# Attention output token-major with a ones column, and one common pool of PSUM banks, in a fused linear-attention and gated-MLP kernel

## The chip, the cores and the metric

The kernel runs on one core of a Trainium2 chip. The metric is the device time of one execution in microseconds (us). The kernel before took 319.83 us (median of three runs, 319.49 to 319.84) when the prediction was made.

The engines go by the names of the profile: PE is TensorE, which multiplies matrices (PEld is its loading of weights), DVE is VectorE, ACT is ScalarE, POOL is GpSimd. Of the two operands of a matmul, the one that is loaded as weights is called stationary here, the other moving. PSUM (PS in the profiles) is the memory that the matmuls of this kernel write to; the kernel uses it as eight banks.

## The reference, cut to what matters

```python
xn = layernorm(x)                                  # x: 2048 tokens x 640
q, k, v = split(xn @ wqkv)                         # 32 heads of 20
pq, pk = q @ w_phi, k @ w_phi                      # per head, 20 x 20
phi_q = concat(softmax(pq), softmax(-pq))          # same for phi_k with pk
kv = phi_k^T @ v ;  z = sum over tokens of phi_k   # per head
o = (phi_q @ kv) / (phi_q @ z + 1e-6)
out = x + o @ wo + (silu(xn @ w1) * (xn @ w3)) @ w2    # hidden width 1536
```

There are two halves that share the normalised tokens: a linear attention, and a gated MLP that is by far the larger part of the matmul work.

## The kernel before

The program is written as *streams* of steps: norms, attention, k normalisations, MLP, output tiles. When it is built, a small recorder looks at the head of every stream, estimates with its own costs when each could start, and commits the one that could start first; ties go to the earlier stream. The result is a fixed order of instructions on each engine, with semaphore waits.

The step that normalises k is a DVE reduction and reciprocal, and two POOL multiplications. The kv sums need all of them:

```python
def k_norm(t):                                         # (cut: the names of views)
    P.op("DVE", "tensor_reduce", [s], [e], ...)        # sums of exp over each head
    P.op("DVE", "reciprocal", [r], [s], ...)
    for sg in range(2):                                # sg: exp(pk), exp(-pk)
        tt("POOL", ev, ev, r[...].to_broadcast(...), ALU.mult)

def kv_sum(sg, fc, k):                                 # (cut: h0, h1, nh, the heads of this chunk)
    for t in range(T):
        mm(bank(k, 21 * nh), ekt[:, t, sg, fc * 128:(fc + 1) * 128],
           v2[:, t, 21 * h0:21 * (h1 + 1)], t == 0, t == T - 1)
    # ... masked copies of the result into KVc (kv) and ZG (z)
```

The attention output works on 512 tokens with channels on the partitions. The softmax sums and the denominators are found token-major, turned around, spread over the channels by a matmul with a 0/1 matrix (GT2), and multiplied onto exp(pq) before the product with kv:

```python
def q_sums(b, k):
    for j in range(4):
        for sg in range(2):
            for fc in range(DC):
                mm(bank(k, 64, 128 * j + 64 * sg), EqT[...][:, sg, fc, 128 * j:128 * j + 128],
                   ZG[:, sg, fc, :], fc == 0, fc == DC - 1)
    # ... DVE: products, sum, reciprocal, g_s
def q_scale_t(b, k):                       # four transposes of g_s, ACT copy to gT
def q_scale(b, fc, k):
    for r, sg in ((0, 1), (1, 0)):
        mm(bank(k + r), GT2[32 * r:32 * r + 32, ...], gT[32 * r:32 * r + 32, b % 2, :], True, True)
    for r, sg in ((0, 1), (1, 0)):
        tt("DVE", e, e, bank(k + r), ALU.mult)          # 128 x 512
def q_out(b, dc, k):                       # 26 matmuls of 512 columns for a block
    for n, (sg, fc) in enumerate(plan):
        mm(bank(k), KVc[:, sg, fc, dc * 128:(dc + 1) * 128], EqT[b % 2][:, sg, fc, :], ...)
```

The eight PSUM banks are two rings of four, A for the attention and M for the MLP and the output tiles:

```python
def banks(stream, n):
    base, size = {"A": (0, 4), "M": (4, 4)}[stream]
    # ... next n banks of that ring
```

An MLP chunk is ten matmuls of 512 columns, a tanh on ACT and two operations on DVE. There are 48 chunks; block 2 may be computed before the kv sums, block 3 only after them (its output lies over data that the kv sums read):

```python
while done["t"] < 4 * b + 4 or b == 2 and done["t"] < T or b == 3 and not done["kv"]:
    yield None
yield lambda b=b, fc=fc: mlp(b, fc, banks("M", 2))
```

The softmax here doesn't subtract the row's maximum and nothing guards it: scores larger than these inputs give would overflow.

## Time and profile before

| engine | busy, us of 316.6 | share |
|---|---|---|
| PE (matmuls) | 300.7 | 95% |
| DVE | 177.6 | 56% |
| ACT | 118.5 | 37% |
| POOL | 67.2 | 21% |

First, the page of the kernel before: the span, the busy time of each engine, and the chain of work that ended last, by engine and line with shares of the span.

```profile
span 316.6 us, 4949 instructions
...
PE 300.7 (95%) x2088; PEld 178.8 (56%) x2114; DVE 177.6 (56%) x292; ACT 118.5 (37%) x195; POOL 67.2 (21%) x89
...
PE 94%; DMA 2%; ACT 1%; DVE 1%; issue 1%; SPq 0%
```

The chain is TensorE from end to end. Whether its engine is really never idle is read in the table of waits of PE: who it waited for, in total, how many times, and the longest.

```profile
PE PS L101 <- DVE x_tok L101: 8.3, 2, 5.9
PE PS L101 <- ACT v_84 L101: 1.5, 3, 0.5
PE PS L101 <- ACT ekt L101: 1.1, 1, 1.1
...
PE PS L101 <- DVE ZG L101: 0.2, 1, 0.2
```

Apart from the load of the first tokens there are about 3 us of waits. So the time is the sum of the matmuls, and the sizes that count are distances from start to start. They are read in the timeline (start, length, what, how many; PS is PSUM, w_s the MLP weights, xnT the normalised tokens turned around, Wqp and Wkp the weights of the q and k projections), because the length of a row includes the tail of its last matmul. For that reason the busy time of PE is not a measure of closeness to a limit either; the Trainium skill, "Trainium Kernel Development and Optimization", "Performance Expectations", says so ("a bad metric"), and this trace agrees: one 512-column matmul is listed with 379 ns, while ten of them take 2.16 us.

```profile
144.06 10.83 PE L101 MATMUL PS<-v_84,ekt 128*128 128x147 bf16 x160
154.72 0.43 PE L101 MATMUL PS<-ZG,EqT_74 128*128 128x64 bf16 x9
...
182.39 1.33 PE L101 MATMUL PS<-ZG,EqT_80 128*128 128x64 bf16 x40
183.77 5.34 PE L101 MATMUL PS<-xnT,Wqp 128*128 128x512 bf16 x24
...
191.65 0.60 PE L101 MATMUL PS<-gT,GT_51 32*128 32x512 bf16 x4
192.19 4.49 PE L101 MATMUL PS<-xnT,w_s 128*128 128x512 bf16 x19
...
257.11 5.56 PE L101 MATMUL PS<-EqT_80,KVc 128*128 128x512 bf16 x25 [0.16 <-issue]
262.51 1.52 PE L101 MATMUL PS<-wo_s,oT 128*128 128x320 bf16 x10
```

The reader sees 10.66 us for the 160 kv sums (66.6 ns each), 1.38 us for the forty z matmuls of a block, 0.54 us for four scale matmuls, and 5.40 us for the 26 output matmuls of a block (one record is missing in that row).

### The profile page before, as it was taken

How to read it: one execution, taken by the hardware profiler on the slowest of the kernel's cores; microseconds unless marked ns; L12 is line 12 of the kernel's file. 1: busy time of each engine (PE TensorE's matmuls, PEld its weight loads, DVE VectorE, ACT ScalarE, POOL GpSimd, SP SyncE). 2: the span in 40 equal slices, each digit the busy share in tenths (PEclk: the TensorE clock that was granted, in tenths of full speed). 3: DMA queues.
4: the chain of work that ended last, by engine and by line, in shares of the span. 5: the costliest groups of instructions: out<-in, count | busy, mean ns of one | idle time of the engine just before them, and what ended most of it. 6: DMA issues, size and time to landing. Idle time of an engine off the chain costs nothing.

```text
span 316.6 us, 4949 instructions
## 1 busy us (share of the span) xinstructions
PE 300.7 (95%) x2088; PEld 178.8 (56%) x2114; DVE 177.6 (56%) x292; ACT 118.5 (37%) x195; POOL 67.2 (21%) x89
## 2 busy tenths in 40 slices
PE   0799999999999799999999999999999999999996
PEld 0465655555555456448844453454557656777774
DVE  3866476789877877774339538753743651112212
ACT  2476675757444555540172373346030010000000
POOL 4621032447533375990000000000000000000000
PEclk9999999999999999999999999999999999999999
DMA  7996000000000300000360000000011120222211
GB/s 245 339 356 204 2 1 1 3 0 2 0 0 2 97 9 0 1 2 0 93 222 0 0 2 0 0 3 0 3 41 43 49 76 5 80 85 63 63 62 41
DMA packets 15542, 17.38 MB, mean 55 GB/s; under 512 B 1440, under 2 KB 15520, under 8 KB 15520
## 3 DMA queue, kind: packets, MB, share of 16 engines
q1 hardware_dynamic: 15520, 17.07, 17.0%
q8 instruction: 16, 0.26, 0.3%
q14 instruction: 6, 0.05, 0.0%
HBM read 14.44 MB, written 2.62 MB: 54 GB/s over the span
## 4 chain that ended last, share of the span: by engine, by line
PE 94%; DMA 2%; ACT 1%; DVE 1%; issue 1%; SPq 0%
PE PS L101 94%; DMA x_tok<-in_A_x_dram 2%; ACT v_84 L101 1%; ACT ekt L101 0%; SPq L113 0%; DVE bst L101 0%; DVE xres L101 0%; DVE x_tok L101 0%; DVE KVc L101 0%; DVE mv L101 0%; DVE ZG L101 0%
## 5 line engine op out<-in xcount | busy, mean ns | idle before, releaser
L101 PE MATMUL PS<-xnT,w_s 128*128 128x512 bf16 x460 | 106.5, 379 | 1.1
L101 PEld LDWEIGHTS PS<-xnT,w_s 128*128 128x128 bf16 x480 | 45.3, 98 | 51.0 <-issue 1.3
L101 DVE SCALAR_TENSOR_TENSOR t_66<-th,PS 128x512 bf16<-128x512 f32 x48 | 32.8, 683 | 46.6 <-ACT th L101 46.6
L101 POOL TENSOR_TENSOR ekt<-ekt,rS_60 128x640 bf16<-128x640 bf16 x32 | 39.8, 1269 | 50.2 <-DVE rS_60 L101 50.2
L101 DVE TENSOR_TENSOR xres<-PS,xres 128x640 bf16<-128x640 f32 x16 | 13.2, 824 | 53.8 <-PE PS L101 53.8
L101 ACT ACTIVATE th<-PS 128x512 f32<-128x512 f32 x48 | 28.8, 600 | 32.3 <-PE PS L101 31.8
L101 ACT ACTIVATE ekt<-PS 128x640 bf16<-128x640 f32 x32 | 20.8, 701 | 23.5 <-PE PS L101 23.5
L101 PE MATMUL PS<-wv,xnT 128*128 128x320 bf16 x160 | 25.3, 308 | 2.2 <-ACT ekt L101 1.1
L101 PE MATMUL PS<-Wkp,xnT 128*128 128x320 bf16 x160 | 24.2, 299 | 0.5 <-ACT v_84 L101 0.5
L101 PE MATMUL PS<-wo_s,oT 128*128 128x320 bf16 x160 | 24.4, 299 | 0.0
L101 DVE TENSOR_REDUCE S_59<-ekt 128x64 f32<-128x1280 bf16 x16 | 23.4, 1465 | 0.0
L101 ACT ACTIVATE oT<-PS 128x512 bf16<-128x512 f32 x14 | 8.4, 597 | 40.0 <-PE PS L101 40.0
L101 PEld LDWEIGHTS PS<-wv,xnT 128*128 128x128 bf16 x160 | 15.9, 101 | 10.5 <-ACT v_84 L101 1.4
L101 PE MATMUL PS<-xnT,Wqp 128*128 128x512 bf16 x96 | 21.4, 379 | 0.2
L101 PEld LDWEIGHTS PS<-Wkp,xnT 128*128 128x128 bf16 x160 | 15.5, 98 | 8.7 <-ACT v_84 L101 0.7
L101 PEld LDWEIGHTS PS<-wo_s,oT 128*128 128x128 bf16 x160 | 15.3, 98 | 7.2 <-issue 0.8
L101 DVE BATCH_NORM_STATS2 bst<-x_tok 128x6 f32<-128x320 bf16 x32 | 15.3, 479 | 4.5 <-DMA x_tok<-in_A_x_dram 3.9
L101 ACT ACTIVATE v_84<-PS 128x640 bf16<-128x640 f32 x16 | 11.3, 707 | 15.5 <-PE PS L101 15.4
L101 PEld LDWEIGHTS PS<-xnT,Wqp 128*128 128x128 bf16 x100 | 9.5, 98 | 11.1
L101 PE MATMUL PS<-ident,x_tok 128*128 128x128 bf16 x80 | 7.6, 230 | 8.3 <-DVE x_tok L101 8.3
L101 PE MATMUL PS<-w_s,hT_75 128*128 128x320 bf16 x96 | 13.7, 299 | 0.0
L101 PE MATMUL PS<-w_s,hT_76 128*128 128x320 bf16 x96 | 13.7, 299 | 0.0
(75 smaller groups left out, 342.7 us busy)
## 6 DMA issues: line engine op xcount, KB each, us to landing
w_s<-in_B_w_dram SPq DMA_DIRECT2D x6, 640.0 KB, 10.2
xres<-in_A_x_dram SPq DMA_DIRECT2D x16, 160.0 KB, 2.4
out_dram<-xres SPq DMA_DIRECT2D x16, 160.0 KB, 1.8
x_tok<-in_A_x_dram SPq DMA_DIRECT2D x3, 640.0 KB, 8.8
w_s<-in_B_w_dram SPq DMA_DIRECT2D x1, 1920.0 KB, 7.9
wqk_s<-in_A_wqkv_dram SPq DMA_DIRECT2D x2, 800.0 KB, 8.7
wv<-in_A_wqkv_dram SPq DMA_DIRECT2D x1, 800.0 KB, 4.8
wo_s<-in_A_wo_dram SPq DMA_DIRECT2D x1, 800.0 KB, 4.6
```

The lines of the kernel that those rows point to most:

```text
L101: o = _Op(eng, lambda: m(*args, **kw), r, w, cost)
```

## The change

Its intent is to make the attention output token-major. exp(pq) becomes the stationary operand and kv the moving one, with z and a ones column beside each head, so that numerators, denominators and softmax sums come out of the same matmuls. DVE divides, the two signs are added, and o is turned by five PE transposes. Each output product of 128 tokens needs four PSUM banks at once, so the two rings of banks become one common pool, in which each step takes the group that is estimated to be free first.

```diff
-    def q_sums / q_scale_t / q_scale / q_out      (cut: removed whole)
+    def q_tok(t, k):
+        for sg in range(2):
+            for fc in range(DC):
+                for q in range(2):                       # two halves of the heads, one bank each
+                    ...
+                        mm(bank(k + 2 * sg + q, 22 * (hi - lo), 22 * (lo - 16 * q)),
+                           EqT[b % 2][:, sg, fc, 128 * j:128 * j + 128],
+                           KVc[:, sg, fc, 22 * (lo - h0):22 * (hi - h0)], ...)
+        ...                                              # ACT: two copies of sums and denominators
+        tt("DVE", pr, e[:, 0:2, :], e[:, 2:4, :], ALU.mult)
+        tt("DVE", den, pr[:, 0, :], pr[:, 1, :], ALU.add)
+        P.op("DVE", "reciprocal", [den], [den], (den, den), cost=0.42)
+        tt("DVE", g, e[:, 2:4, :], den..., ALU.mult)
+        tt("DVE", p2..., ps[:, :, :, 0:DH], g..., ALU.mult)            # 1280 elements from PSUM
+        tt("DVE", o_tok[:, t % 3, :], p2[:, 0, :], p2[:, 1, :], ALU.add, 2)
+    def o_transpose(t, k):                               # five transposes, one copy to oT
-    def banks(stream, n):                                # two rings of four
+    def banks(n):
+        def free_at(k): ...                              # estimated end of the last use
+        return min(range(0, 8, n), key=free_at)
-    kv_init, GT2, ZG                                     (cut: zero fills and the 0/1 matrix go)
+    streams = [norms(), attention(), k_norms(), o_transposes(), mlps(), outs()]
```

More of the change, by code (lines that the diff above doesn't have):

```diff
@@ L274, in bass_parallel_sum__linear_kernel_hedgehog__glu_gated_swiglu__prompt_kernel @@
     GM = new("GM", [128, DC, H], bf)
-    GT2 = new("GT2", [64, D], bf)
     phi_s = new("phi_s", [128, DC, DH], bf)
@@ L282, in bass_parallel_sum__linear_kernel_hedgehog__glu_gated_swiglu__prompt_kernel @@
     warm = new("warm", [128, 8], f32)
+    pr_s = new("pr_s", [128, 2, 2, H], f32)
+    den_s = new("den_s", [128, 2, H], f32)
+    g_s = new("g_s", [128, 2, 2, H], f32)
     S64 = new("S64", [128, 3, 64], f32)
@@ L296, in bass_parallel_sum__linear_kernel_hedgehog__glu_gated_swiglu__prompt_kernel @@
     wo_s = new("wo_s", [128, DC, D], bf, RX + 12288)
-    ZG = new("ZG", [128, 2, DC, 64], bf, RX + 18688)
     RKV = region(12800)
@@ L312, in bass_parallel_sum__linear_kernel_hedgehog__glu_gated_swiglu__prompt_kernel @@
     EqT1 = new("EqT1", [128, 2, DC, 512], bf, RE + 27648)
-    E_s = new("E_s", [128, 4, 128], f32, RE + 37888)
-    den_s = new("den_s", [128, 4, 32], f32, RE + 39936)
     wqk_s = new("wqk_s", [128, DC, 2 * D], bf, RE + 40960 - 12800)
@@ L320, in bass_parallel_sum__linear_kernel_hedgehog__glu_gated_swiglu__prompt_kernel @@
     oT = new("oT", [128, DC, S], bf, RV)
+    e_s = new("e_s", [128, 2, 4, H], f32, RV + 20480)
     RW = region(12800)
     wqkT = new("wqkT", [128, 2 * DC, D], bf, RW)
-    KVc = new("KVc", [128, 2, DC, D], bf, RW)
+    KVc = new("KVc", [128, 2, DC, 8 * 22], bf, RW)
+    prod = new("prod", [128, 2, 2, D], bf, RW + 3520)
+    o_tok = new("o_tok", [128, 3, D], bf, RW + 8640)
     EqT = [EqT0, EqT1]
-    gT = new("gT", [64, 2, 512], bf, RKV + 10240)
-    g_s = new("g_s", [128, 4, 64], bf, RKV + 12288)
-    pr_s = new("pr_s", [128, 4, 64], f32, RV + 20480)
     PS = nc.alloc_psum_tensor("PS", [128, 8 * 512], f32)
@@ L431, in consts_late @@
         memset("POOL", v2[:].rearrange("p t (h c) -> p t h c", c=21)[:, :, :, DH], 1.0)
-        memset("POOL", GT2[:], 1.0)
-        for r in (0, 32):
-            select(GT2[r:r + 32, :], 0, [[1, D]], -DH, ALU.is_ge, 0.0)
-            select(GT2[r:r + 32, :], DH, [[-1, D]], DH, ALU.is_gt, 0.0)
     def ln_stats(t0, n):
@@ L535, in kv_sum @@
         g = GM[:, fc, h0:h1 + 1]
-        tt("DVE", KVc[:, sg, fc, DH * h0:DH * (h1 + 1)].rearrange("p (h k) -> p h k", k=DH),
-           pv[:, :, 0:DH], g.unsqueeze(2).to_broadcast([128, nh, DH]), ALU.mult)
-        stt(ZG[:, sg, fc, 32 * sg + h0:32 * sg + h1 + 1], pv[:, :, DH],
-            DEN_EPS if sg == 0 else 0.0, g, ALU.add, ALU.mult)
-    def kv_init():
-        memset("POOL", KVc[:], 0.0)
-        memset("POOL", ZG[:], 0.0)
-        copy("POOL", ZG[:, 0, :, 32:64], GM[:])
-        copy("POOL", ZG[:, 1, :, 0:32], GM[:])
+        kv = KVc[:, sg, fc, 0:22 * nh].rearrange("p (h c) -> p h c", c=22)
+        tt("DVE", kv[:, :, 0:DH], pv[:, :, 0:DH], g.unsqueeze(2).to_broadcast([128, nh, DH]), ALU.mult)
+        stt(kv[:, :, DH], pv[:, :, DH], DEN_EPS if sg == 0 else 0.0, g, ALU.add, ALU.mult)
+        copy("POOL", kv[:, :, DH + 1], g)
     def q_proj(b, fc, k):
@@ L553, in q_proj @@
         act(EqT[b % 2][:, 1, fc, :], bank(k), ACT.Exp, -1.0)
-    def q_sums(b, k):
-        for j in range(4):
-            for sg in range(2):
-                for fc in range(DC):
-                    mm(bank(k, 64, 128 * j + 64 * sg), EqT[b % 2][:, sg, fc, 128 * j:128 * j + 128],
-                       ZG[:, sg, fc, :], fc == 0, fc == DC - 1)
-        copy("ACT", E_s[:], bank(k).rearrange("p (j c) -> p j c", c=128))
-        tt("DVE", pr_s[:], E_s[:, :, 0:64], E_s[:, :, 64:128], ALU.mult)
-        tt("DVE", den_s[:], pr_s[:, :, 0:32], pr_s[:, :, 32:64], ALU.add)
-        P.op("DVE", "reciprocal", [den_s[:]], [den_s[:]], (den_s[:], den_s[:]), cost=1.2)
-        tt("DVE", g_s[:].rearrange("p j (s h) -> p j s h", h=32),
-           E_s[:, :, 32:96].rearrange("p j (s h) -> p j s h", h=32),
-           den_s[:].unsqueeze(2).to_broadcast([128, 4, 2, 32]), ALU.mult)
@@ L570, in q_scale_t @@
-    def q_scale_t(b, k):
-        for j in range(4):
-            tr(PSb[0:64, k * 1024 + 128 * j:k * 1024 + 128 * j + 128], g_s[:, j, :])
-        copy("ACT", gT[:, b % 2, :], PSb[0:64, k * 1024:k * 1024 + 512])
-    def q_scale(b, fc, k):
-        for r, sg in ((0, 1), (1, 0)):
-            mm(bank(k + r), GT2[32 * r:32 * r + 32, fc * 128:(fc + 1) * 128],
-               gT[32 * r:32 * r + 32, b % 2, :], True, True)
-        for r, sg in ((0, 1), (1, 0)):
-            e = EqT[b % 2][:, sg, fc, :]
-            tt("DVE", e, e, bank(k + r), ALU.mult)
@@ L584, in q_out @@
-    def q_out(b, dc, k):
-        plan = []
-        for fc in range(DC):
-            h0, h1 = heads_of_chunk(fc)
-            if max(128 * dc, DH * h0) < min(128 * dc + 128, DH * h1 + DH):
-                plan += [(0, fc), (1, fc)]
-        for n, (sg, fc) in enumerate(plan):
-            mm(bank(k), KVc[:, sg, fc, dc * 128:(dc + 1) * 128], EqT[b % 2][:, sg, fc, :],
-               n == 0, n == len(plan) - 1)
-        evac(oT[:, dc, b * 512:(b + 1) * 512], bank(k))
+    def q_tok(t, k):
+        b, j = divmod(t, 4)
+        for sg in range(2):
+            first = [True, True]
+            for fc in range(DC):
+                h0, h1 = heads_of_chunk(fc)
+                for q in range(2):
+                    lo, hi = max(h0, 16 * q), min(h1 + 1, 16 * q + 16)
+                    if lo < hi:
+                        mm(bank(k + 2 * sg + q, 22 * (hi - lo), 22 * (lo - 16 * q)),
+                           EqT[b % 2][:, sg, fc, 128 * j:128 * j + 128],
+                           KVc[:, sg, fc, 22 * (lo - h0):22 * (hi - h0)],
+                           first[q], fc == DC - 1 or (q == 0 and fc == 2), True)
+                        first[q] = False
+        ps = PS[:, k * 512:(k + 4) * 512].rearrange("p (n c) -> p n c", c=512)[:, :, 0:352]
+        ps = ps.rearrange("p n (h c) -> p n h c", c=22)
+        e = e_s[:, t % 2, :, :]
+        for sg in range(2):
+            act(e[:, sg:4 - sg:3 - 2 * sg, :].rearrange("p c (q h) -> p q h c", h=16),
+                ps[:, 2 * sg:2 * sg + 2, :, 20:22], ACT.Copy)
+        pr, den, g = pr_s[:, t % 2, :, :], den_s[:, t % 2, :], g_s[:, t % 2, :, :]
+        tt("DVE", pr, e[:, 0:2, :], e[:, 2:4, :], ALU.mult)
+        tt("DVE", den, pr[:, 0, :], pr[:, 1, :], ALU.add)
+        P.op("DVE", "reciprocal", [den], [den], (den, den), cost=0.42)
+        tt("DVE", g, e[:, 2:4, :], den.unsqueeze(1).to_broadcast([128, 2, 32]), ALU.mult)
+        g = g.rearrange("p s (q h) -> p (s q) h", h=16)
+        p2 = prod[:, t % 2, :, :]
+        tt("DVE", p2.rearrange("p s (q h c) -> p (s q) h c", q=2, c=DH), ps[:, :, :, 0:DH],
+           g.unsqueeze(3).to_broadcast([128, 4, 16, DH]), ALU.mult)
+        tt("DVE", o_tok[:, t % 3, :], p2[:, 0, :], p2[:, 1, :], ALU.add, 2)
@@ L596, in bass_parallel_sum__linear_kernel_hedgehog__glu_gated_swiglu__prompt_kernel @@
+    def o_transpose(t, k):
+        for dc in range(DC):
+            tr(PSb[:, k * 1024 + 128 * dc:k * 1024 + 128 * dc + 128],
+               o_tok[:, t % 3, 128 * dc:128 * dc + 128])
+        src = PSb[:, k * 1024:k * 1024 + D].rearrange("p (c n) -> p c n", n=128)
+        evac(oT[:, :, t * 128:(t + 1) * 128], src)
     nmlp = [0]
@@ L625, in out_tile, with free_at @@
         finish.append(P.dma("SP", out_t[:, t, :], xres[:, t % 4, :]))
-    turn = {"A": 0, "M": 0}
-    def banks(stream, n):
-        base, size = {"A": (0, 4), "M": (4, 4)}[stream]
-        p = turn[stream]
-        if n > 1 and p % n:
-            p += n - p % n
-        turn[stream] = p + n
-        return base + p % size
-    done = dict.fromkeys(("ln", "t", "k", "n", "kv", "o", "h"), 0)
+    def banks(n):
+        def free_at(k):
+            return max([o.end for i in range(k, k + n) for o in P.bank.get(("P", i), {}).values()],
+                       default=0.0)
+        return min(range(0, 8, n), key=free_at)
+    done = dict.fromkeys(("ln", "t", "k", "n", "kv", "q", "o", "h"), 0)
     def norms():
@@ L672, in transposed @@
             yield None
-        yield lambda: xn_transpose(t, banks("A", 1))
+        yield lambda: xn_transpose(t, banks(1))
         done["t"] = t + 1
@@ L680, in attention @@
                 yield from transposed(t + 1)
-            yield lambda t=t: v_tile(t, banks("A", 2))
+            yield lambda t=t: v_tile(t, banks(2))
         for e in range(DC):
-            yield lambda e=e: fold_t(1, e, banks("A", 1))
+            yield lambda e=e: fold_t(1, e, banks(1))
         for dc in range(DC):
-            yield lambda dc=dc: fold_mm(1, dc, banks("A", 2))
+            yield lambda dc=dc: fold_mm(1, dc, banks(2))
         for t in range(T):
-            yield lambda t=t: k_tile(t, banks("A", 2))
+            yield lambda t=t: k_tile(t, banks(2))
             done["k"] = t + 1
@@ L691, in attention @@
             if t >= 4:
-                yield lambda t=t: v_tile(t, banks("A", 2))
+                yield lambda t=t: v_tile(t, banks(2))
             if 4 <= t < 9:
-                yield lambda e=t - 4: fold_t(0, e, banks("A", 1))
+                yield lambda e=t - 4: fold_t(0, e, banks(1))
             if 9 <= t < 14:
-                yield lambda dc=t - 9: fold_mm(0, dc, banks("A", 2))
-        yield kv_init
+                yield lambda dc=t - 9: fold_mm(0, dc, banks(2))
         yield lambda: P.dma("SP", wo_s[:], A_wo.rearrange("(c p) d -> p c d", p=128))
         for fc in range(DC):
-            yield lambda fc=fc: q_proj(0, fc, banks("A", 1))
+            yield lambda fc=fc: q_proj(0, fc, banks(1))
         while done["n"] < T:
@@ L704, in attention @@
             for sg in range(2):
-                yield lambda fc=fc, sg=sg: kv_sum(sg, fc, banks("A", 1))
+                yield lambda fc=fc, sg=sg: kv_sum(sg, fc, banks(1))
         done["kv"] = 1
@@ L709, in attention, with o_transposes @@
         for b in range(NB):
-            yield lambda b=b: q_sums(b, banks("A", 1))
-            if b + 1 < NB:
-                for fc in range(DC):
-                    yield lambda b=b, fc=fc: q_proj(b + 1, fc, banks("A", 1))
-            yield lambda b=b: q_scale_t(b, banks("A", 1))
-            for fc in range(DC):
-                yield lambda b=b, fc=fc: q_scale(b, fc, banks("A", 2))
-            for dc in range(DC):
-                yield lambda b=b, dc=dc: q_out(b, dc, banks("A", 1))
-            done["o"] = b + 1
+            for j in range(4):
+                t = 4 * b + j
+                yield lambda t=t: q_tok(t, banks(4))
+                done["q"] = t + 1
+                if b + 1 < NB:
+                    for fc in range((5 * j + 3) // 4, (5 * j + 8) // 4):
+                        yield lambda b=b, fc=fc: q_proj(b + 1, fc, banks(1))
+    def o_transposes():
+        for t in range(T):
+            while done["q"] <= t:
+                yield None
+            yield lambda t=t: o_transpose(t, banks(1))
+            done["o"] = t + 1
     def mlps():
@@ L725, in mlps @@
                     yield None
-                yield lambda b=b, fc=fc: mlp(b, fc, banks("M", 2))
+                yield lambda b=b, fc=fc: mlp(b, fc, banks(2))
             done["h"] = b + 1
@@ L730, in outs @@
         for t in range(T):
-            while done["o"] <= t // 4 or done["h"] <= t // 4:
+            while done["o"] <= t or done["h"] <= t // 4:
                 yield None
-            yield lambda t=t: out_tile(t, banks("M", 2))
-    streams = [norms(), attention(), k_norms(), mlps(), outs()]
+            yield lambda t=t: out_tile(t, banks(2))
+    streams = [norms(), attention(), k_norms(), o_transposes(), mlps(), outs()]
     n = len(streams)
@@ L748, in bass_parallel_sum__linear_kernel_hedgehog__glu_gated_swiglu__prompt_kernel @@
                 continue
-            save = dict(turn), nmlp[0], len(finish)
+            save = nmlp[0], len(finish)
             ops = P.step(heads[i])
-            after = dict(turn), nmlp[0], finish[save[2]:]
-            turn.update(save[0])
-            nmlp[0] = save[1]
-            del finish[save[2]:]
+            after = nmlp[0], finish[save[1]:]
+            nmlp[0] = save[0]
+            del finish[save[1]:]
             if any(o.eng == "PE" for o in ops):
@@ L765, in bass_parallel_sum__linear_kernel_hedgehog__glu_gated_swiglu__prompt_kernel @@
         at, i, ops, after = best
-        turn.update(after[0])
-        nmlp[0] = after[1]
-        finish.extend(after[2])
+        nmlp[0] = after[0]
+        finish.extend(after[1])
         P.commit(ops)
```

## The prediction

> **What bounds it now.** TensorE. On the profile page PE is busy 300.7 of 316.6 us (95%), DVE 56%, ACT 37%, POOL 21%, granted clock 0.998. The chain of waits is 94% PE matmuls. The table of waits gives PE about 11 us of idle time: 8.3 us for the first normalised tokens (load time), 2.6 us for ACT to free PSUM banks (v 1.5, ekt 1.1), 0.2 for the kv evacuation.
>
> **Removed, PE** (start to start in the timeline, per block of 512 tokens): 26 output matmuls of 512 columns 5.40 us; 10 scale-expansion matmuls 1.38 us (0.53 per four: they run in pairs); 40 z matmuls of 64 columns 1.38 us; 4 transposes of the scales 0.34 us. Sum 8.5, times 4 = 34.0 us, plus 0.4 us of small bubbles. DVE loses 24.8 us of scale multiplications.
>
> **Added, PE.** Per 128 tokens 8 matmuls of 154 and 4 of 88 columns. The kv sums (147 to 168 columns, new weights each) run 66 ns apart, the 64-column ones 34 ns, so about 66 and 40 ns: 0.69 us, times 16 = 11.0 us. Five transposes run 0.28 us in the xn stage: 4.5 us. Net -18.9 us, all critical.
>
> **DVE.** Per 128 tokens: three tiny tensor_tensors and a reciprocal, estimate 1.0 us (from 292 ns at 128 elements; reciprocal 553 at 64), the 1280-element product from PSUM 1.49 us (824 ns at 640), the bf16 addition 0.49 us if it runs at two per cycle (the Trainium skill, "VectorE: DVE Perf Modes", perf-mode tier table, gives tensor_tensor 2x for bf16 in SBUF; no tensor_tensor of this trace shows it). About 3.0 us, 48 us in all. While MLP chunks (1.37 us of DVE each) fill between, DVE has about 4.4 us per 4.3 to 6.5 us of PE: tight, 1 to 2 us of PE stalls. Later, between output tiles (4.6 us PE, 0.82 us DVE), no stall.
>
> **Common pool.** The 2.6 us of waits for ACT largely vanish. But the order moves: K/V stage without MLP between, then 33 MLP chunks in one row. The last two k normalisations stand on DVE behind the 33rd chunk. From the last MLP matmul: DVE tail 1.1 us, then reduce 1.465 + reciprocal 0.553 each, POOL four multiplications of 1.27: the last is ready about 8.3 us on, while the kv sums have only about 2 us of work that can run. Nothing else may run (the last MLP block waits for kv). A new PE bubble of about 6 us, in two gaps of 3.5 and 2.5 us. The Trainium skill, "TensorE: Matmul & The Clock Gate", Part 1, says about 3.4 us of idleness can halve the clock; the ten wv matmuls after the start-up idle took 2.65 us against 1.53 later, which agrees. I count 1 us. The K/V stage loads ACT to about 90% of PE: 1 us.
>
> **Sum:** 319.8 - 34.4 + 15.5 - 2.6 + 6 + 1 + 1 + 1.5 = 307.8; I take 307 us, 301 to 313. Faster by over 2% 0.92, within 2% 0.07, slower 0.01.
>
> **Right or wrong shows as:** PE busy about 280 us; 154- and 88-column groups near 11 us start to start; DVE busy 190 to 205 us; waits of PE on POOL ekt about 6 us, just before the kv sums; PE waits on ACT v/ekt below 1 us; in the q stage PE waits on DVE prod/o_tok below 3 us.
>
> **What would break it:** DVE chain holding four banks so that PE stalls over 5 us in the q stage; the product at under one element per cycle; the K/V stage ACT- or POOL-bound (over 5 us idle); slow clock after the bubble; or the bubble filled (then 301).

## More of the kernel before

The kv sums begin at once behind the MLP.

## The result, and the profile after

The changed kernel takes 307.15 us (median of four runs, 306.27 to 307.80) against 319.69 us in the same session. The ratio is 0.9606 with a 95% interval of 0.9578 to 0.9634.

The page of the changed kernel, the same lines:

```profile
span 305.8 us, 4978 instructions
...
PE 286.2 (94%) x2066; PEld 181.9 (59%) x2066; DVE 191.6 (63%) x335; ACT 118.4 (39%) x212; POOL 59.1 (19%) x90
...
PE 92%; DVE 3%; DMA 2%; POOL 1%; ACT 1%; issue 0%; SPq 0%
```

Its waits of PE:

```profile
PE PS L101 <- DVE x_tok L101: 9.4, 2, 5.9
PE PS L101 <- POOL ekt L101: 5.7, 2, 3.5
PE PS L101 <- ACT EqT_81 L101: 0.8, 1, 0.8
PE PS L101 <- DVE prod L101: 0.6, 1, 0.6
```

The waits for ACT at v and ekt are gone, and a wait for POOL is there that the kernel before did not have. Where it stands, and what the new products cost, is in its timeline of PE:

```profile
149.42 1.06 PE L101 MATMUL PS<-v_83,ekt 128*128 128x147 bf16 x14
153.96 0.24 PE L101 MATMUL PS<-v_83,ekt 128*128 128x147 bf16 x1 [3.48 <-POOL ekt L101]
156.41 12.59 PE L101 MATMUL PS<-v_83,ekt 128*128 128x147 bf16 x145 [2.21 <-POOL ekt L101]
168.84 2.32 PE L101 MATMUL PS<-xnT,w_s 128*128 128x512 bf16 x10
171.00 0.85 PE L101 MATMUL PS<-KVc,EqT_75 128*128 128x154 bf16 x12
171.69 2.32 PE L101 MATMUL PS<-xnT,Wqp 128*128 128x512 bf16 x10
...
177.78 0.44 PE L101 MATMUL PS<-ident,o_tok 128*128 128x128 bf16 x5
178.06 2.32 PE L101 MATMUL PS<-xnT,w_s 128*128 128x512 bf16 x10
...
221.51 0.86 PE L101 MATMUL PS<-KVc,EqT_75 128*128 128x154 bf16 x12 [0.59 <-DVE prod L101]
```

An output product takes 0.69 us and five transposes 0.28 us, as estimated. The kv sums have two holes near their start, 3.48 and 2.21 us. They are also slow themselves: the last 145 take 12.43 us (156.41 to 168.84), 86 ns each, where the kernel before needs 66.6 ns. At 66.6 ns they would take 9.66 us, so 2.8 us are lost. The windows view gives the clock that was granted to TensorE (PEclk, as a share of the full one). It has 0.82 in that stretch and 1.00 in the five others that cover the rest of the span; cut finer, the stretch shows half clock for 6.8 us (the last three lines).

```profile
core 0: us, PE busy (x) PEld busy (x) DVE busy (x) ACT busy (x) POOL busy (x), PEclk, DMA share, GB/s
...
149.40:168.90 19.50, 13.80 (x162) 13.45 (x161) 9.48 (x24) 0.00 (x0) 6.84 (x13) 0.82 0.00 1
...
149.40:155.40 6.00, 1.32 (x16) 0.96 (x14) 4.99 (x6) 0.00 (x0) 2.76 (x3) 1.00 0.00 0
155.40:162.20 6.80, 5.79 (x48) 5.79 (x49) 1.48 (x6) 0.00 (x0) 2.78 (x5) 0.50 0.00 0
162.20:168.90 6.70, 6.70 (x101) 6.70 (x100) 3.01 (x12) 0.00 (x0) 1.30 (x6) 1.00 0.01 2
```

From 156.41 to 162.2 us the kv sums ran at half clock. Half of these 5.8 us is 2.9 us, which is the loss. The 1.00 of the view says nothing of the very start: the clock records of this trace begin at 15.4 us only.

Why POOL is late is in its own timeline. It did nothing for 69.87 us and then got the last two k normalisations at the moment when TensorE needed them:

```profile
152.64 4.95 POOL L101 TENSOR_TENSOR ekt<-ekt,rS_62 128x640 bf16<-128x640 bf16 x4 [69.87 <-DVE rS_62 L101]
```

The reason, as read from the code of the recorder, is this. Whenever it has committed an MLP chunk, its estimate for DVE ends later than that for PE, because the tail of the chunk is on DVE. A k normalisation can start only where DVE is free, the next MLP chunk already where PE is free, so the MLP chunk wins 33 times in a row, and the last two normalisations are committed when the chunks have run out. In the kernel before, the rings of banks kept the MLP chunks scattered over the K/V stage, and the last normalisation was ready 1.4 us before the MLP chunks ran out (POOL ended at 142.7 us, the kv sums began at 144.06).

The DVE groups of the changed kernel (count, busy us and mean ns of one, idle before) confirm the estimated durations of the division chain:

```profile
L101 DVE TENSOR_TENSOR prod<-PS,g_s 128x1280 bf16<-128x1280 f32 x16 | 23.9, 1491 | 0.5
L101 DVE TENSOR_TENSOR o_tok<-prod 128x640 bf16<-128x640 bf16 x16 | 7.9, 492 | 0.5
```

### The profile page after: what moved, and what is told of

Same layout as the page of the kernel before. It is cut to its first block, busy times and chain, and to the rows that moved or that the text cites. A ratio compares the mean times of both kernels' runs of the same rounds, so it can differ in the third digit from the quotient of the medians.

```text
span 305.8 us, 4978 instructions
## 1 busy us (share of the span) xinstructions
PE 286.2 (94%) x2066; PEld 181.9 (59%) x2066; DVE 191.6 (63%) x335; ACT 118.4 (39%) x212; POOL 59.1 (19%) x90
## 4 chain that ended last, share of the span: by engine, by line
PE 92%; DVE 3%; DMA 2%; POOL 1%; ACT 1%; issue 0%; SPq 0%
PE PS L101 92%; DMA x_tok<-in_A_x_dram 2%; POOL ekt L101 1%; DVE prod L101 0%; DVE S_61 L101 0%; SPq L113 0%; ACT EqT_81 L101 0%; DVE bst L101 0%; DVE xres L101 0%; DVE t_68 L101 0%; ACT th L101 0%; DVE den_s L101 0%; DVE rS_62 L101 0%; DVE x_tok L101 0%; ACT e_s L101 0%
## 5 line engine op out<-in xcount | busy, mean ns | idle before, releaser
L101 PEld LDWEIGHTS PS<-xnT,w_s 128*128 128x128 bf16 x480 | 46.4, 98 | 54.1 <-ACT EqT_75 L101 0.3
L101 PE MATMUL PS<-wv,xnT 128*128 128x320 bf16 x160 | 26.3, 316 | 0.0
L101 DVE TENSOR_TENSOR prod<-PS,g_s 128x1280 bf16<-128x1280 f32 x16 | 23.9, 1491 | 0.5
L101 PE MATMUL PS<-xnT,Wqp 128*128 128x512 bf16 x100 | 23.7, 379 | 0.0
L101 ACT ACTIVATE e_s<-PS 128x64 f32<-128x64 f32 x32 | 9.1, 283 | 37.3 <-PE PS L101 36.3
L101 PE MATMUL PS<-v_83,ekt 128*128 128x147 bf16 (+1 forms) x160 | 13.9, 259 | 5.7 <-POOL ekt L101 5.7
L101 PEld LDWEIGHTS PS<-v_83,ekt 128*128 128x128 bf16 x160 | 13.5, 113 | 6.3 <-POOL ekt L101 6.0
```

The costliest lines, as they stand in the source:

```text
L101: o = _Op(eng, lambda: m(*args, **kw), r, w, cost)
```

## The experiments

Twelve kernels ran, all with correct results. Theory 1 says: the matmuls saved are worth what the starts in the timeline say; the pool, by changing the order, costs a hole at the kv sums; and the slow kv sums behind it are the clock. The rivals: the gain comes from the pool; POOL is too slow for any such order; the slow kv sums wait for data.

| run | time, us | ratio to before | 95% interval |
|---|---|---|---|
| after_again | 306.04 | 0.9566 | 0.9538 to 0.9595 |
| knorm_earlier | 305.77 | 0.9566 | 0.9536 to 0.9595 |
| gap_filled | 313.49 | 0.9810 | 0.9783 to 0.9838 |
| pool_alone | 323.50 | 1.0115 | 1.0086 to 1.0144 |
| attention_alone | 321.97 | 1.0067 | 1.0038 to 1.0095 |
| pool_alone_knorm_earlier | 318.08 | 0.9929 | 0.9908 to 0.9949 |
| product_twice | 315.98 | 0.9865 | 0.9843 to 0.9887 |
| knorm_earlier_warm_start | 296.07 | 0.9237 | 0.9215 to 0.9259 |
| spaced | 305.94 | 0.9551 | 0.9527 to 0.9575 |
| knorm_earlier_spaced | 296.56 | 0.9267 | 0.9247 to 0.9286 |
| gap_filled_spaced | 303.86 | 0.9490 | 0.9467 to 0.9513 |
| attention_alone_spaced | 314.00 | 0.9811 | 0.9780 to 0.9842 |

The first four shared one call (before: 319.69 us), the next four another (320.22), the last four a third (320.11). Across calls, compare ratios.

### The changed kernel again: after_again

No edit.

> The changed kernel once more, as the yardstick of this call: 306 to 308 us, ratio to before 0.958 to 0.963; two TensorE gaps of about 3.5 and 2.2 us at the start of the kv sums, and the kv sums after them at about 86 ns each instead of the 66 ns of before.

It took 306.04 us, with the same two holes (3.49 and 2.22 us). The ratio, 0.9566, lies a little below the range expected, 0.958 to 0.963: so much does one kernel differ.

### The k normalisations earlier: knorm_earlier

```diff
-                while done["t"] < 4 * b + 4 or b == 2 and done["t"] < T or b == 3 and not done["kv"]:
+                while done["t"] < 4 * b + 4 or b == 2 and (done["t"] < T or fc >= 6 and done["n"] < T) or b == 3 and not done["kv"]:
```

The last six MLP chunks of block 2 are held back until all k normalisations are recorded.

> The last two k normalisations are recorded six MLP chunks earlier; nothing else changes. Theory 1 (the hole at the kv sums is made by those two normalisations standing behind the 33rd MLP chunk on DVE, and the slow kv sums after it are the clock falling because of the hole): both gaps go (5.7 us) and the kv sums return to 66 ns each (2.8 us), so 8.5 us less than the changed kernel: 298 to 300 us, ratio to before about 0.934. Rival (POOL is simply too slow for this order, so the wait moves to another place): less than 3 us gained, and PE waits for POOL or DVE elsewhere.

A miss: 305.77 us, no gain. But the timeline of PE shows that the first half came true, and where it was lost:

```profile
143.28 10.83 PE L101 MATMUL PS<-v,ekt 128*128 128x147 bf16 x160
...
156.10 0.85 PE L101 MATMUL PS<-KVc,EqT 128*128 128x154 bf16 x12
...
227.71 1.60 PE L101 MATMUL PS<-KVc,EqT 128*128 128x154 bf16 x24
231.59 0.86 PE L101 MATMUL PS<-KVc,EqT 128*128 128x154 bf16 x12 [2.28 <-DVE prod L101]
234.65 1.50 PE L101 MATMUL PS<-KVc,EqT 128*128 128x154 bf16 x12 [2.19 <-DVE prod L101]
237.71 2.85 PE L101 MATMUL PS<-wo_s,oT 128*128 128x320 bf16 x10 [1.56 <-DVE prod L101]
```

The kv sums have no hole and run at 66.6 ns. The first output product starts at 156.10 us. In the changed kernel it starts at 171.00, with three more MLP chunks (6.5 us) done by then, so 8.4 us were gained up to there. The gain was given back in the last block: from 227.71 us, four output products stand next to each other. Two of them hold all eight banks, and each later one waits until the DVE product of an earlier one has freed four banks. These waits are 6.0 us, and the matmuls behind them are slow (1.50 us for twelve instead of 0.85, 2.85 for ten instead of 1.52; the granted clock is 0.50 from 234.2 to 241.0 us), which costs about 2.3 us more. In the recorder this arrangement keeps itself up: when four banks come free, a product and an output tile could both start, and the tie goes to the product, whose stream comes first. That last sentence is read from the code; that the neighbourhood costs the time is tested with the runs called spaced.

### TensorE busy in the hole: gap_filled

```diff
+    def fill(n, k):
+        for i in range(n):
+            mm(bank(k), xnT[:, 0, 0:128], xnT[:, i % DC, 0:512], True, True)
+        yield lambda: fill(26, banks(1))          # in front of the kv sums
```

> The changed kernel with 26 matmuls of 512 columns on unused data (5.6 us, result never read) in front of the kv sums. The hole stays, only TensorE is busy in it. Theory 1 (the slow kv sums after the hole are the clock): they run at 66 ns, and 2.5 to 3 us are gained, about 304.3 us. Rival (they wait for POOL or their own data): still about 86 ns, no gain, or a loss of up to 1 us.

A miss in time, 313.49 us. The kv sums did go fast (145 in 10.1 us), and the first product started at 168.36 instead of 171.00 us. But this recording, too, had four products side by side from 239.8 us on, with 6.0 us of waits for DVE prod.

### The pool alone: pool_alone

```diff
 # the kernel before, old attention
-    def banks(stream, n):                      # two rings of four
+    def banks(stream, n):
+        def free_at(k): ...                    # as in the change
+        return min(range(0, 8, n), key=free_at)
 # (cut: the recorder's saving of the ring positions goes)
```

> The kernel before with the common pool of PSUM banks alone, the old attention. Theory 1: PE waits for ACT at v and ekt (1.6 us in the K/V stage) go, but the MLP chunks move in one row behind the K/V stage too, and here one k normalisation stands behind the last chunk: a gap of about 3.3 us and slow kv sums for about 2 us; sum 319.7 - 2 + 3.3 + 2 = 323 us, ratio 1.005 to 1.015. Rival (the pool is a gain by itself): 317 to 318 us, ratio below 0.995.

323.50 us, 1.2% slower than before, as expected by theory 1. The MLP chunks move behind the K/V stage here too, one k normalisation stands behind the last of them, and the timeline shows the hole and the slow kv sums:

```profile
149.81 1.12 PE L101 MATMUL PS<-v,ekt 128*128 128x147 bf16 x15
154.36 11.53 PE L101 MATMUL PS<-v,ekt 128*128 128x147 bf16 x145 [3.42 <-POOL ekt L101]
```

So the common pool by itself is a loss, and the gain of the change is not its gain. The rival falls. (That the hole is what makes it a loss is shown by pool_alone_knorm_earlier below.)

### The attention alone: attention_alone

```diff
 # the changed kernel
-    def banks(n): ...                          # common pool
+    def banks(n, stream="A"): ...              # two rings of four, as before; MLP and output tiles take "M"
 # (cut: the recorder saves the ring positions again)
```

> The token-major attention with the old two pools of four banks; each output product then takes all four banks of its pool. Theory 1 (the matmuls saved are worth 18.9 us, and the pool is needed only to keep two output products in flight): no hole at the kv sums (no k normalisation stands behind the last chunk), but in the last block four output products follow each other with nothing between and each waits for the DVE chain of the one before (about 3.3 us from the last matmul to the banks free): 10 to 14 us of PE waits for DVE prod. Sum 319.7 - 18.9 + 12 = 313 us, 310 to 316. Rival (the gain comes from the pool): no better than before.

A miss: 321.97 us, slower than before. The timeline of its end shows why. Output tiles ran ahead, two to a product, and in the last block none was left to put between:

```profile
282.09 1.50 PE L101 MATMUL PS<-KVc,EqT 128*128 128x154 bf16 x12 [3.03 <-DVE prod L101]
...
291.16 1.50 PE L101 MATMUL PS<-KVc,EqT 128*128 128x154 bf16 x12 [3.03 <-DVE prod L101]
296.21 2.32 PE L101 MATMUL PS<-ident,o_tok 128*128 128x128 bf16 x20 [3.56 <-DVE o_tok L101]
```

The left-out row between is one more of the same kind. Here one product fills its ring, and the next waits out the whole DVE chain. In all there are 16.9 us of waits for DVE (prod 12.1, o_tok 3.6, oT 1.2). The 12.1 us for prod are what I had counted; the others, and the slow matmuls behind all but the first of these waits, I had not (the granted clock is 0.50 for 23.9 us in all).

### The pool alone, k normalisations earlier: pool_alone_knorm_earlier

The edit of knorm_earlier on pool_alone.

> The old attention with the common pool and the k normalisations recorded earlier. If the hole is what the pool costs, its removal leaves the pool worth 1 to 3 us: 316.5 to 319 us, ratio 0.99 to 0.998; and no gap at the kv sums. If it stays above 321 us the cost of the pool lies elsewhere.

318.08 us, as expected: no hole at the kv sums, which run at 66.7 ns. Without the hole the pool is worth 0.7%, about 2.3 us, which is the size of the waits for ACT that it takes away.

### The DVE product twice: product_twice

```diff
+        again = ...                              # output and inputs of the product above
+        P.op("DVE", "tensor_tensor", [again[0]], list(again[1:]), (*again, ALU.mult), cost=0.0)
```

The product is repeated with the same operands, and the recorder is told that it costs nothing, so that the order stays (it moved in one place, by one MLP chunk).

> The changed kernel with the 1280-element DVE product done twice (16 x 1.49 = 23.9 us of DVE more; the same values, so still right). If DVE had slack throughout (rival): under 1.5 us more. My theory: while MLP chunks fill (first eight products) DVE is near its limit, so that about half of those eight show: 6 us more, between 3 and 10; PE waits for DVE prod or for hT of that size.

315.98 us. By the ratios (0.9865 against 0.9566 to 0.9606 for the changed kernel) that is 8 to 10 us more for 23.9 us of DVE work. It is at the upper end of what I expected: the DVE chain is not slack. The line of its waits of PE that grew (it was 0.6 us in the changed kernel):

```profile
PE PS L101 <- DVE prod L101: 5.7, 6, 2.1
```

Of these 5.7 us, 3.6 came in five waits with MLP chunks between the products, and 2.1 behind the ninth product.

### Earlier k normalisations and a warm start: knorm_earlier_warm_start

```diff
 # on knorm_earlier
+    def warm_pe(n, k):
+        for i in range(n):
+            mm(bank(k), hT0[:, 0, 0:128], hT0[:, 0, :], True, True)     # zeros
     def attention():
+        yield lambda: (memset("DVE", hT0[:, 0, :], 0.0), warm_pe(8, 7))
         yield from transposed(0)
+        yield lambda: warm_pe(16, 7)
```

> knorm_earlier plus 24 matmuls of zeros while the first tokens load, so that TensorE is not idle before the first v tiles. If the slow first v tiles (2.67 and 2.14 us for ten matmuls instead of 1.36) are the clock as at the kv sums: they run in about 1.36 us and 1.5 to 2.3 us are gained over knorm_earlier, about 297 us. If they are bound by the loads (DMA): no gain, the time is only moved into waits for x_tok or wv.

296.07 us, the lowest time. Two things came together here. The additional matmuls also changed the recording, and this time an output tile stood between the products of the last block, so the 8.5 us of knorm_earlier showed. The share of the warm start itself is read at the beginning of its timeline:

```profile
1.29 3.39 PE L101 MATMUL PS<-hT 128*128 128x512 bf16 x8 [1.29 <-DVE hT L101]
...
6.14 3.62 PE L101 MATMUL PS<-hT 128*128 128x512 bf16 x16
...
10.68 1.52 PE L101 MATMUL PS<-wv,xnT 128*128 128x320 bf16 x10
12.03 0.44 PE L101 MATMUL PS<-ident,x_tok 128*128 128x128 bf16 x5
```

The first eight filler matmuls take about 420 ns each, the next sixteen 216 ns, and the first ten v matmuls 1.35 us from start to start. In the changed kernel these took 2.67 us. From the first v matmul to the end of the v tiles it is 6.0 us, against 8.3 us in knorm_earlier_spaced below, so the beginning was 2.3 us shorter. In time the two cannot be told apart well: 0.9237 and 0.9267 come with intervals that overlap.

### An output tile between two products: spaced, and the three repeats

```diff
+                while t > 8 and done["out"] == seen:
+                    yield None
                 yield lambda t=t: q_tok(t, banks(4))
+                seen = done["out"]
```

This rule makes the recorder place an output tile between two products from the tenth on. For attention_alone, an output tile must in addition wait until the product eight tiles ahead is recorded, so that tiles do not run out.

> The changed kernel with a rule in the recording that an output tile stands between two output products from the tenth on (the changed kernel breaks it only once, where it waits 0.6 us for DVE prod). Yardstick for the next two: the holes at the kv sums stay; 305 to 307 us, ratio 0.953 to 0.962.

> knorm_earlier again with the same rule. If the missing gain of knorm_earlier is only that four products of the last block stood next to each other with nothing between (6.0 us of PE waits for DVE prod, and a slow clock behind them), the full 8.5 us shows now: 297 to 299 us, ratio about 0.932, PE waits for DVE prod below 1 us, clock back at 1.0. If it stays above 303 us, something else took the gain.

> gap_filled again with the same rule: the POOL wait stays, TensorE only works on unused data through it. If the clock is what slows the kv sums, 2.5 to 3 us less than spaced: 302.5 to 304 us, ratio about 0.949. If not, the same as spaced.

> attention_alone with the rule, and output tiles not running ahead, so that one stands behind each of the last nine products. If the loss of attention_alone was the run of products at its end (about 17 us of PE waits and a slow clock), it is now faster than before in spite of the small pools: 309 to 314 us; each product still needs all four banks of its pool, so 5 to 10 us of waits for DVE prod or ACT stay. If the attention were no gain without the pool, it would stay at 318 us or more.

spaced took 305.94 us: by itself the rule changes nothing that can be told from the scatter.

knorm_earlier_spaced took 296.56 us, 9.4 us less than spaced; 8.5 were expected. PE waits for nothing but the first tokens (9.7 us), and the mean clock is back at 1.0. So theory 1 holds for the hole, and the rival (POOL too slow) falls: POOL does the same work in the same time, only earlier. The run also tests the matmuls saved. Against pool_alone_knorm_earlier it differs in the attention and in the rule of spaced, which is worth nothing by itself: by the ratios (0.9929 and 0.9267) that is 21 us. In the two traces the matmuls that were exchanged differ by 18.7 us from start to start, where 18.9 were counted; the rest is smaller waits and gaps.

gap_filled_spaced took 303.86 us, 2.1 us less than spaced (2.5 to 3 expected). The timeline shows the filler and the kv sums behind it:

```profile
149.28 5.78 PE L101 MATMUL PS<-xnT 128*128 128x512 bf16 x26
154.89 1.13 PE L101 MATMUL PS<-v,ekt 128*128 128x147 bf16 x15
156.29 10.08 PE L101 MATMUL PS<-v,ekt 128*128 128x147 bf16 x145 [0.27 <-POOL ekt L101]
166.20 2.32 PE L101 MATMUL PS<-xnT,w_s 128*128 128x512 bf16 x10
```

The data came no earlier (156.29 instead of 156.15 us in spaced), yet the same 145 matmuls took 9.91 us instead of 12.35. The granted clock was 1.00 throughout that stretch. So they were slowed by the clock that the idleness before them had lowered, not by their data.

attention_alone_spaced took 314.00 us (309 to 314 expected), 1.9% faster than before and 8 us faster than attention_alone (by the ratios). The new attention is a gain with the old rings too, once its products are kept apart. It keeps 11.3 us of waits (ACT EqT 5.9, DVE prod 3.0, ACT oT 2.4): each product takes the whole ring of four, so the q projection and the transposes, which need banks of the same ring, stand in its way. With the common pool (knorm_earlier_spaced) none of these waits is left.

## Why the prediction was right

The predicted time, 307 us, is the measured one, 307.15 us. The mechanism was right: the matmuls saved, the hole, its cause. That the numbers meet within 0.2 us is partly luck, because the terms were not all as good as the sum and their errors cancel.

| term, as predicted | us | measured in the profile |
|---|---|---|
| old output, z, scale matmuls and transposes removed | -34.4 | gone from the timeline; in the trace before, their distances from start to start add up to 34.5 us |
| 16 products of 0.69 us | +11.0 | 0.69 us each (171.00 to 171.69), 11.05 us in all |
| 16 times five transposes | +4.5 | 0.28 us each (177.78 to 178.06), but 0.39 in the last block (243.15 to 243.54): 5.1 us in all |
| waits for ACT at v and ekt vanish | -2.6 | gone; pool_alone_knorm_earlier puts the pool at -2.3 us |
| hole at the kv sums | +6 | 3.48 + 2.21 = 5.7 us |
| slow clock behind it | +1 | 2.8 us |
| K/V stage near the limit of ACT | +1 | no PE wait in that stage |
| waits in the q stage | +1.5 | 0.59 + 0.76 = 1.35 us |

- **The saved matmuls** were right, because they were costed from start to start in the trace. Taken from lengths, one 512-column matmul would have been 379 ns instead of 216. The two kernels without holes, pool_alone_knorm_earlier and knorm_earlier_spaced, confirm them (18.7 us).
- **The hole** was right in size, place and its division in two. It could be predicted only from the order of the built program: the diff says nothing of it. knorm_earlier_spaced shows the cause.
- **The clock** was right in kind and mis-sized: 2.8 us instead of 1. The Trainium skill, "TensorE: Matmul & The Clock Gate", Part 1, says that the clock is halved after a window of about 3.4 us of idleness, and that it takes about as long of activity to come back. Half clock stands behind the holes (0.50 from 155.4 to 162.2 us), it is gone when the holes are filled (gap_filled_spaced), and the full clock came back 2.7 us (product_twice) to 5.8 us after the kv sums had begun again. How long it lasts is not fixed by the holes: with the same two holes product_twice has 0.50 for 3.4 us only, and its 145 kv sums take 10.98 us, a loss of 1.3 us instead of 2.8. In pool_alone the clock fell about 1 us after the hole of 3.42 us was over (0.50 from 155.3 to 158.7 us), a loss of 1.7 us. The prediction gives no working for its 1 us.
- **The DVE chain** was right: 2.98 us for one tile of 128 tokens in the trace (224 + 191 + 353 + 225 + 1491 + 492 ns), 3.0 predicted. The doubled rate that the Trainium skill, "VectorE: DVE Perf Modes", in the perf-mode tier table gives for a bf16 tensor_tensor in SBUF agrees with the trace: 492 ns for 640 elements, against 825 ns for the 640-element addition that reads PSUM. An estimate from these: the forms that read PSUM take 825 ns for 640 and 1491 ns for 1280 elements, so 1.04 ns for each and 159 ns besides; with the same 159 ns, the bf16 addition takes 0.52 ns for each.
- **The place of the q-stage waits** was wrong, though the sum was right. The step "Later, between output tiles (4.6 us PE, 0.82 us DVE), no stall" failed: with MLP chunks between there was no wait at all, and the 1.35 us came behind the ninth product, where no output tile or chunk stood between two products. At this load of DVE the neighbourhood of products decides; with more load (product_twice) waits come between MLP chunks as well. The prediction compared busy times there. It named a DVE chain that holds four banks as a risk, but not what brings it about: two products with nothing between fill all eight banks.
- **PE busy** came out at 286.2 us and not at about 280: busy time also counts matmuls that are slow. 300.7 us less 34.5, plus 16.1 for the products and transposes, plus 2.8 for the slow kv sums and about 1 for slow v tiles, gives it.
- **Not in the sum:** the first tokens. PE waited 9.4 us for them and not 8.3. But 9.3 to 10.6 us are read in every other profile with an unfilled start, the old attention with the common pool included (10.3), so this is not of the change.

On the spans of the two profiles (316.6 and 305.8 us) the measured terms give -34.5 + 16.1 - 2.6 + 5.7 + 2.8 + 1.4 = -11.1 us, and the later and slower first v tiles add about 2 us: -9.1, where -10.8 is observed. The rest is small gaps of the kernel before: PE was idle for 15.9 us of its span, 11.4 in the waits of its table and 3.1 behind the last matmul, so 1.4 us in gaps too small for the table. In the changed kernel no such rest is left (19.6 = 16.5 + 3.1). Another 0.5 us are the waits for ZG and issue, which are gone too, so that the account closes to 0.2 us. The medians of the session differ by more, 12.5 us, because the profiled execution of the kernel before (318.32 us) was 1.4 us quicker than its median.

My first experiments missed where the prediction had not. In knorm_earlier and gap_filled I expected the edited place alone to change, and the recorder made a new order in a place that I had not touched. Reading the order of the edited kernels to the end before running them would have shown the products side by side. In attention_alone I had foreseen the products side by side, but not the waits for o_tok and oT and the slow clock that came with them.

## What to carry to other kernels

Where one engine bounds a kernel, cost a change from start to start in that engine's timeline, and then read the new order of instructions to its end: what stands in front of the instruction that everything waits for matters as much as the work removed. Here a shared pool of buffers was worth 0.7% to the old attention (pool_alone_knorm_earlier), and more to the new one, whose products take four banks at once (296.6 us with it in knorm_earlier_spaced, 314.0 without in attention_alone_spaced); but with it a rule was needed that keeps such steps apart, and one that lets short steps on the way to a barrier go first. Two such rules, a few lines each, brought 307 us to 296.6 us (the ratio from 0.9606 to 0.9267); neither alone gained anything that can be told from the scatter (spaced 305.94, knorm_earlier 305.77).

## What the Trainium skill lacked or had wrong

- "TensorE: Matmul & The Clock Gate", Part 1: it gives a window of about 3.4 us of idleness, and for frequent shorter gaps no number. Here waits of 2.28 and 2.19 us with one product between (knorm_earlier) were followed by twelve matmuls in 1.50 instead of 0.85 us, and waits of 3.03 us (attention_alone) likewise.
- The same page gives as remedy a loop without gaps, and a warm-up for benchmarks. No page says what filling a gap with unused matmuls brings: 26 of them in a hole of 5.7 us saved 2.1 us (gap_filled_spaced), and 24 in the load time at the start made the beginning 2.3 us shorter (knorm_earlier_warm_start).
- The same page, Part 2, "Back-to-back issue gap", puts a sustained stream of weight loads and matmuls at about 81 ns for 128 columns, against about 56 ns without them. Here 128-column transposes, each with its own weight load, stand 56 ns apart, and matmuls of 147 to 168 columns 66.6 ns.
